# QK and exp cut into score chunks, set between AV and the MLP's matmuls

## The chip, the cores and the metric

The kernel runs on one core of a Trainium2 chip. A core has engines that run side by side, each with its own queue of instructions: TensorE (PE in the profile; its weight loads are the row PEld), VectorE (DVE), ScalarE (ACT), GpSimd (POOL), and SyncE (SP), which here only starts DMA transfers. They wait for one another through semaphores. Matmul results go to PSUM, everything else lies in SBUF.

The metric is the device time of one execution in microseconds (us). The time before is 412.74 us, the median of 6 runs (411.07 to 414.85).

## The reference

Grouped-query attention, then a gated MLP with a spatial mix. Cut to what is computed:

```python
# q: (8, 16, 384, 64)   k, v: (8, 4, 384, 64)    B, heads, S, D
k = np.repeat(k, 4, axis=1); v = np.repeat(v, 4, axis=1)
scores = (1 / np.sqrt(64)) * np.matmul(q, k.transpose(0, 1, 3, 2))
scores = scores - np.max(scores, axis=-1, keepdims=True)
attn = np.exp(scores)
attn = attn / (np.sum(attn, axis=-1, keepdims=True) + 1e-09)
x = np.matmul(attn, v).transpose(0, 2, 1, 3).reshape(8, 384, 1024)

h = np.maximum(x @ w_in, 0.0)                 # w_in: 1024 x 1024
u, v = h[..., :512], h[..., 512:]
v_n = (v - mean(v)) / np.sqrt(var(v) + 1e-06)
v_s = np.einsum('ts,bsd->btd', w_spatial, v_n) + b_spatial[None, :, None]
out = (u * v_s) @ w_out                       # w_out: 512 x 1024
```

## The kernel before

All 8 batches run on the one core, in a software pipeline of three stages: pass `it` does the attention of batch b0 = it, the normalization of the attention result and the first half of the MLP of batch b1 = it - 1, and the second half of the MLP of batch b2 = it - 2. A list `sched` gives the order of the pieces; a framework adds the semaphores. The order in the list is the order of preference: the framework may let a later instruction pass an earlier one on the same engine.

Heads are taken in pairs; a "unit" u is the heads 2u and 2u + 1, which share one k and v with the next or the previous unit. The scores stand transposed, 384 keys by 384 queries, as three chunks c of 128 keys. The pieces that matter:

```python
def psum_t(name):                      # every PSUM tile is one of 8 buffers
    return pp.tile([P, DH], FP32, name=name, tag="u", bufs=8)

def a_tr(b, u):                        # load and transpose q (and k, every second unit)
    ...
        nc.tensor.transpose(pkt[:, c * P:(c + 1) * P], k_sb[:, c], ident)      # x3
    nc.vector.tensor_copy(out=kT2, in_=pkt[:, 0:S])
    nc.gpsimd.dma_start(out=v_ext[:, :, 0:D], in_=v[b, hkv]...)                # 2 buffers
    ...
        nc.tensor.transpose(pqt[:, c * P:(c + 1) * P], q_sb[:, c], ident)      # x3
    nc.vector.tensor_copy(out=qT2, in_=pqt[:, 0:S])

def a_qk(b, u):                        # all scores of both heads, then all exps
    for c in range(NSC):               # NSC = 3
        for jj in range(2):            # D = 64 rows each, the two heads side by side
            lo = jj * D
            ps = psum_t(f"psc{jj}")
            pscs[jj][c] = ps
            nc.tensor.matmul(ps[:, 0:S], kT2[lo:lo + D, c * P:(c + 1) * P],
                             qT2[lo:lo + D, :], start=True, stop=True)
    for jj in range(2):
        p_sb = sb.tile([P, NSC, S], A, name="p_sb", tag="p_sb", bufs=8)
        for c in range(NSC):
            nc.scalar.activation(out=p_sb[:, c, :], in_=pscs[jj][c][:, 0:S],
                                 func=EXP, scale=scale)

def a_av(b, u):                        # v times exp, with a row of ones for the sum
    for jj in range(2):
        pav = psum_t("pav")
        for c in range(NSC):
            nc.tensor.matmul(pav[0:D + 1, 0:S], v_ext[:, c], p_sb[:, c],
                             start=(c == 0), stop=(c == NSC - 1))
        nc.vector.tensor_copy(out=st[b]["av"][0:D + 1, h, :], in_=pav[0:D + 1, 0:S])

def a_tail(b):                         # the sums of all heads, to 16 rows and back
    nc.sync.dma_start(out=dcol, in_=av_all[D:D + 1, :, :])
    nc.vector.reciprocal(out=rcol, in_=dcol)
    nc.sync.dma_start(out=rrow, in_=rcol)

def a_evac(b, hh):                     # four heads: broadcast 1/sum, multiply
    for h in range(hh, hh + 4):
        nc.gpsimd.partition_broadcast(R, rrow[:, h * S:(h + 1) * S], channels=D)
        nc.vector.tensor_tensor(out=st[b]["xT"][h // 2][lo:lo + D, :], ..., op=MULT)
```

`g_u` (x @ w_in, left half, 2 of 4 column blocks), `g_v` (right half, one of 3 row blocks), `g_n` (normalization), `g_s` (spatial mix, 2 of 4 blocks: matmuls `pvs`, then `gT` = `pvs` times u on VectorE) and `g_o` (@ w_out, one of 3 row blocks) are the MLP. The order of one pass:

```python
sched = [
    (a_tr, b0, 0), (a_tail, b1, None),
    (a_tr, b0, 1), (a_qk, b0, 0),
    (a_tr, b0, 2), (a_qk, b0, 1),
    (a_tr, b0, 3), (a_av, b0, 0), (a_qk, b0, 2), (a_evac, b1, 0),
    (a_tr, b0, 4), (a_av, b0, 1), (a_qk, b0, 3), (a_evac, b1, 4),
    (g_s, b2, 0),
    (a_tr, b0, 5), (a_av, b0, 2), (a_qk, b0, 4), (a_evac, b1, 8),
    (g_s, b2, 2),
    (a_tr, b0, 6), (a_av, b0, 3), (a_qk, b0, 5), (a_evac, b1, 12),
    (g_o, b2, 0),
    (a_tr, b0, 7), (a_av, b0, 4), (a_qk, b0, 6),
    (g_u, b1, 0), (g_o, b2, 1),
    (a_av, b0, 5), (a_qk, b0, 7),
    (g_u, b1, 2), (g_o, b2, 2),
    (a_av, b0, 6), (g_v, b1, 0), (g_v, b1, 1),
    (a_av, b0, 7), (g_v, b1, 2), (g_n, b1, None),
]
if it == 0:      # the first pass also loads the weights, and transposes w_spatial (9 blocks)
    sched = sched[0:1] + [(load_weights, 1, None)] + sched[1:9] + \
        [(load_wsp, 1, None)] + sched[9:]
```

The lines of the list are called steps 0 to 10 below (`g_s` and `g_o` belong to the step ahead of them): step s begins with the transposes of unit s.

Of the kernel before, what the change touches and what calls it, by code (L numbers as in the profile page):

```python
# [12 lines left out]
EXP = mybir.ActivationFunctionType.Exp  # L13
# [7 lines left out]
def kernel(  # L21
# [11 lines left out]
    nc = tc.nc  # L33
    P = 128
    B, HQ, S, D = q.shape
# [5 lines left out]
    NSC = S // P  # L41
    NDM = DM // P
    NDD = DH // P
    scale = float(D) ** -0.5
    A = FP16
# [3 lines left out]
    sb = ctx.enter_context(tc.tile_pool(name="sb", bufs=2))  # L49
    pp = ctx.enter_context(tc.tile_pool(name="pp", bufs=1, space=bass.MemoryType.PSUM))  # L50

    def psum_t(name):
        return pp.tile([P, DH], FP32, name=name, tag="u", bufs=8)
# [30 lines left out]
    st = {}  # L84

    def new_batch(b):
        st[b] = {
            "xT": [sb.tile([P, S], A, name=f"xT_{b}_{j}", tag="xT", bufs=2 * NDM)
                   for j in range(NDM)],
            "av": sb.tile([P, HQ, S], A, name="av_all", tag="av_all", bufs=2),  # L90
            "kv": {}, "qT": {}, "p": {}, "uT": [], "vn": [], "gT": [],
            "vsb": [], "acc": [],
        }
# [31 lines left out]
        nc.vector.tensor_copy(out=qT2, in_=pqt[:, 0:S])  # L125
        st[b]["qT"][u] = qT2

    def a_qk(b, u):
        kT2 = st[b]["kv"][u // 2][0]
        qT2 = st[b]["qT"].pop(u)  # L130
        pscs = [[None] * NSC, [None] * NSC]
        for c in range(NSC):
            for jj in range(2):
                lo = jj * D
                ps = psum_t(f"psc{jj}")
                pscs[jj][c] = ps
                nc.tensor.matmul(
                    ps[:, 0:S], kT2[lo:lo + D, c * P:(c + 1) * P], qT2[lo:lo + D, :],
                    start=True, stop=True,
                )  # L140
        for jj in range(2):
            p_sb = sb.tile([P, NSC, S], A, name="p_sb", tag="p_sb", bufs=8)
            st[b]["p"][2 * u + jj] = p_sb
            for c in range(NSC):
                nc.scalar.activation(out=p_sb[:, c, :], in_=pscs[jj][c][:, 0:S],  # L145
                                     func=EXP, scale=scale)

    def a_av(b, u):
        v_ext = st[b]["kv"][u // 2][1]
        for jj in range(2):  # L150
            h = 2 * u + jj
            p_sb = st[b]["p"].pop(h)
            pav = psum_t("pav")
            for c in range(NSC):
                nc.tensor.matmul(  # L155
                    pav[0:D + 1, 0:S], v_ext[:, c], p_sb[:, c],
                    start=(c == 0), stop=(c == NSC - 1),
                )
            nc.vector.tensor_copy(out=st[b]["av"][0:D + 1, h, :],  # L159
                                  in_=pav[0:D + 1, 0:S])  # L160

    def a_tail(b):
        av_all = st[b]["av"]
# [109 lines left out]
    for it in range(B + 2):  # L273
        b0 = it if it < B else None
        b1 = it - 1 if 1 <= it <= B else None
        b2 = it - 2 if it >= 2 else None
        if b0 is not None:
            new_batch(b0)
        sched = [
            (a_tr, b0, 0), (a_tail, b1, None),  # L280
            (a_tr, b0, 1), (a_qk, b0, 0),
            (a_tr, b0, 2), (a_qk, b0, 1),
            (a_tr, b0, 3), (a_av, b0, 0), (a_qk, b0, 2), (a_evac, b1, 0),
            (a_tr, b0, 4), (a_av, b0, 1), (a_qk, b0, 3), (a_evac, b1, 4),
            (g_s, b2, 0),
            (a_tr, b0, 5), (a_av, b0, 2), (a_qk, b0, 4), (a_evac, b1, 8),
            (g_s, b2, 2),
            (a_tr, b0, 6), (a_av, b0, 3), (a_qk, b0, 5), (a_evac, b1, 12),
            (g_o, b2, 0),
            (a_tr, b0, 7), (a_av, b0, 4), (a_qk, b0, 6),  # L290
            (g_u, b1, 0), (g_o, b2, 1),
            (a_av, b0, 5), (a_qk, b0, 7),
            (g_u, b1, 2), (g_o, b2, 2),
            (a_av, b0, 6), (g_v, b1, 0), (g_v, b1, 1),
            (a_av, b0, 7), (g_v, b1, 2), (g_n, b1, None),
        ]
        if it == 0:
            sched = sched[0:1] + [(load_weights, 1, None)] + sched[1:9] + \
                [(load_wsp, 1, None)] + sched[9:]
        for f, b, arg in sched:  # L300
            if b is None:
                continue
            if arg is None:
                f(b)
            else:
                f(b, arg)
# [30 lines left out]
```

The softmax here doesn't subtract the row's maximum and nothing guards it: scores larger than these inputs give would overflow.

## Time and profile before

| | before |
|---|---|
| median of 6 runs | 412.74 us |
| span of the profiled execution | 410.7 us |
| TensorE busy | 337.0 us |
| VectorE busy | 233.2 us |
| ScalarE busy | 213.3 us |
| GpSimd busy | 86.8 us |
| mean granted TensorE clock | 0.908 |

A page of the profile gives the busy time of each engine, then a chain of waits (the work that ended last, followed back), then groups of instructions. A group's line is: source line, engine, operation, output<-inputs, count, busy us and mean ns of one, idle us just before them and what ended it. Tiles are named as in the code: `psc` are scores, `p_sb` the exps, `pav` and `av_all` the AV result in PSUM and in SBUF, `pqt`/`qT` and `pkt`/`kT` the transposed q and k, `Rb` the broadcast reciprocals, `pw` the transposed blocks of w_spatial. The end of a matmul in the profile is modelled and matmuls overlap, so the distance between two starts tells more than a length. The granted clock is a share of full speed. "issue" is time in which an engine waited for nothing that the profile shows.

### The profile page before, as it was taken

The page shows a single profiled execution, that of the slowest core. Times are in us where ns is not written, and L with a number is a line of the kernel's source. Part 1 is how long each engine was busy: PE and PEld are TensorE (multiplying, and loading weights), DVE is VectorE, ACT ScalarE, POOL GpSimd, SP SyncE. Part 2 cuts the span into 40 slices and gives each one's busy share as a digit, 9 for nine tenths or more (in the row PEclk, how much of TensorE's full clock was granted, in tenths as well). Part 3 has the DMA queues.
Part 4 walks back from the last instruction along what each step waited for, and adds up shares of the span by engine and source line. Part 5 has one row for each costly group of instructions (what it writes and reads, how often), then busy time and mean ns, then how long its engine had stood idle before and what let it go on. Part 6 is the DMA issues. An engine that isn't in the chain of part 4 may idle for free.

```text
span 410.7 us, 5629 instructions
## 1 busy us (share of the span) xinstructions
PE 337.0 (82%) x1833; PEld 173.0 (42%) x1833; DVE 233.2 (57%) x593; ACT 213.3 (52%) x500; POOL 86.8 (21%) x179
## 2 busy tenths in 40 slices
PE   0444989898899789978998879978998889849875
PEld 0223545354455444543554445543554445413322
DVE  0211676759933994289617783289717973466240
ACT  1420978439563747557473737557473757303303
POOL 2510202601600070005200150005200340015000
PEclk9855999899999989999899689989899989968968
DMA  4995556116432634344423433354424402101204
GB/s 115 174 202 117 102 100 141 18 19 143 69 124 57 126 61 113 107 96 91 105 78 93 103 56 88 108 103 82 105 78 94 95 6 102 52 4 74 79 0 153
DMA packets 100108, 37.33 MB, mean 91 GB/s; under 512 B 90992, under 2 KB 92400, under 8 KB 100080
## 3 DMA queue, kind: packets, MB, share of 16 engines
q1 hardware_dynamic: 85520, 32.26, 29.9%
q0 software_dynamic: 14560, 4.72, 10.3%
q8 instruction: 14, 0.23, 0.2%
q14 instruction: 14, 0.11, 0.1%
HBM read 28.90 MB, written 12.58 MB: 101 GB/s over the span
## 4 chain that ended last, share of the span: by engine, by line
PE 59%; DVE 19%; ACT 7%; issue 5%; DMA 4%; SPq 3%; POOL 3%; POOLq 0%; ACTq 0%; DVEq 0%
PE pav L155 12%; PE pv L199 10%; PE pu L188 10%; PE po L261 9%; ACT p_sb L145 6%; DVE rcol L168 4%; PE pvs L247 4%; PE pkt L105 3%; PE pqt L123 3%; SPq L117 2%; PE pvs L251 2%; DVE gT L253 2%; DMA wsp_nat<-in_moe_w_spatial_dram 2%; DVE acc L207 1%; POOL Rb L177 1%
## 5 line engine op out<-in xcount | busy, mean ns | idle before, releaser
L159 DVE CAST av_all<-pav 65x384 f16<-65x384 f32 x128 | 67.0, 548 | 57.6 <-PE pav L155 53.7
L155 PE MATMUL pav<-p_sb,v_ext 128*65 128x384 f16 x384 | 81.3, 349 | 0.9 <-DVE av_all L159 0.7
L109 POOL DMA_DIRECT2D v_ext<-in_v_dram x32 | 25.1, 784 | 226.8 <-DVE av_all L159 56.2
L177 POOL PARTITION_BROADCAST Rb<-rrow x128 | 54.1, 543 | 50.9 <-DMA rrow<-rcol 28.2
L155 PEld LDWEIGHTS <-v_ext 128*65 128x65 f16 x384 | 46.2, 121 | 23.2 <-issue 2.6
L267 ACT COPY osb<-po 128x512 f32<-128x512 f32 x48 | 28.2, 593 | 38.2 <-PE po L261 37.6
L123 PE MATMUL pqt<-ident,q_sb 128*128 128x128 f32 x192 | 35.7, 306 | 7.6 <-DMA q_sb<-in_q_dram 7.6
L206 ACT ACTIVATE vsb<-pv 128x512 f16<-128x512 f32 x24 | 14.3, 597 | 40.6 <-PE pv L199 40.6
L123 PEld LDWEIGHTS pqt<-ident,q_sb 128*128 128x128 f32 x192 | 25.3, 158 | 14.4 <-issue 7.8
L207 DVE BATCH_NORM_STATS2 acc<-vsb 128x6 f32<-128x512 f16 x24 | 16.5, 687 | 22.9 <-ACT vsb L206 22.9
L261 PEld LDWEIGHTS <-gT 128*128 128x128 f16 x192 | 19.3, 102 | 23.3 <-issue 5.7
L105 PE MATMUL pkt<-ident,k_sb 128*128 128x128 f32 x96 | 20.2, 327 | 9.5 <-POOL ident masks.py:199 9.4
L193 ACT ACTIVATE uT<-pu 128x384 f32<-128x384 f32 x32 | 16.2, 514 | 11.2 <-PE pu L188 11.2
L113 DVE MEMSET v_ext<- 128x3 f16 x32 | 2.0, 61 | 34.4 <-DMA v_ext<-in_v_dram 34.4
L253 DVE TENSOR_TENSOR gT<-pvs,uT 128x384 f16<-128x384 f32 x32 | 16.7, 553 | 8.1 <-PE pvs L251 7.7
L247 PE MATMUL pvs<-w_spT_88,v_n 128*128 128x384 f16 x32 | 11.9, 372 | 11.2 <-DVE v_n L237 10.6
L105 PEld LDWEIGHTS pkt<-ident,k_sb 128*128 128x128 f32 x96 | 12.2, 160 | 20.1 <-POOL ident masks.py:199 9.4
L168 DVE RECIPROCAL rcol<-dcol 16x384 f16<-16x384 f16 x8 | 20.1, 2516 | 0.0
L261 PE MATMUL po<-w_out_sb_84,gT 128*128 128x512 f16 x48 | 19.4, 404 | 0.3
L261 PE MATMUL po<-w_out_sb_85,gT 128*128 128x512 f16 x48 | 19.2, 400 | 0.0
L261 PE MATMUL po<-w_out_sb_86,gT 128*128 128x512 f16 x48 | 19.0, 397 | 0.0
L261 PE MATMUL po<-w_out_sb_87,gT 128*128 128x512 f16 x48 | 18.9, 393 | 0.0
(1242 smaller groups left out, 740.1 us busy)
## 6 DMA issues: line engine op xcount, KB each, us to landing
q_sb<-in_q_dram SPq DMA_DIRECT2D x128, 96.0 KB, 2.5
out_dram<-osb SPq DMA_DIRECT2D x48, 256.0 KB, 2.0
k_sb<-in_k_dram SPq DMA_DIRECT2D x64, 96.0 KB, 2.5
v_ext<-in_v_dram POOLq DMA_DIRECT2D x32, 48.0 KB, 2.5
wsp_nat<-in_moe_w_spatial_dram SPq DMA_DIRECT2D x9, 64.0 KB, 2.0
w_in_sb_76<-in_moe_w_in_dram POOLq DMA_DIRECT2D x1, 256.0 KB, 4.6
w_in_sb_77<-in_moe_w_in_dram POOLq DMA_DIRECT2D x1, 256.0 KB, 6.3
w_in_sb_78<-in_moe_w_in_dram POOLq DMA_DIRECT2D x1, 256.0 KB, 7.5
```

Source lines behind the costliest of these rows:

```text
L105: nc.tensor.transpose(pkt[:, c * P:(c + 1) * P], k_sb[:, c], ident)
L109: nc.gpsimd.dma_start(out=v_ext[:, :, 0:D], in_=v[b, hkv].rearrange("(shi slo) d -> slo shi d", slo=P),)
L123: nc.tensor.transpose(pqt[:, c * P:(c + 1) * P], q_sb[:, c], ident)
L155: nc.tensor.matmul(pav[0:D + 1, 0:S], v_ext[:, c], p_sb[:, c], start=(c == 0), stop=(c == NSC - 1),)
L159: nc.vector.tensor_copy(out=st[b]["av"][0:D + 1, h, :], in_=pav[0:D + 1, 0:S])
L168: nc.vector.reciprocal(out=rcol, in_=dcol)
L177: nc.gpsimd.partition_broadcast(R, rrow[:, h * S:(h + 1) * S], channels=D)
L188: nc.tensor.matmul(pu[:, 0:S], w_in_sb[dmc][:, ddc * P:(ddc + 1) * P], st[b]["xT"][dmc], start=(dmc == 0), stop=(dmc == NDM - 1),)
L199: nc.tensor.matmul(pv, st[b]["xT"][dmc][:, sc * P:(sc + 1) * P], w_in_sb[dmc][:, DH:DFF], start=(dmc == 0), stop=(dmc == NDM - 1),)
L247: nc.tensor.matmul(pvs[:, 0:S], st[b]["vn"][sc][:, ddc * P:(ddc + 1) * P], w_spT[sc], start=(sc == 0), stop=False,)
L261: nc.tensor.matmul(po, st[b]["gT"][ddc][:, tcn * P:(tcn + 1) * P], w_out_sb[ddc][:, half * DH:(half + 1) * DH], start=(ddc == 0), stop=(dd ...
L267: nc.scalar.copy(out=osb, in_=po)
```

## The change

It cuts the QK block of a unit into its three score chunks. Each chunk computes the two heads' scores (two PSUM tiles and not six) and issues their two exps at once. A pass becomes eleven steps. In step s, chunk 0 of unit s - 1 comes after the transposes of unit s, then AV of unit s - 3, then chunk 1, then what the step has of the MLP and the normalization, then chunk 2. AV takes both heads in turn, chunk by chunk, into two PSUM tiles that are open together. The purpose is that scores, and with them the exps, come in a steadier flow, and that TensorE has AV and MLP work at hand while ScalarE works off the exps. In the first pass the weight loads stand ahead of the first transposes, and the transposes of w_spatial in step 2.

```diff
-    def a_qk(b, u):
+    def a_qk(b, uc):
+        u, c = uc
         kT2 = st[b]["kv"][u // 2][0]
-        qT2 = st[b]["qT"].pop(u)
-        pscs = [[None] * NSC, [None] * NSC]
+        if c == 0:
+            qT2 = st[b]["qT"].pop(u)
+            st[b]["p"][2 * u] = (sb.tile([P, NSC, S], A, name="p_sb", tag="p_sb",
+                                         bufs=8), qT2)
+            st[b]["p"][2 * u + 1] = (sb.tile([P, NSC, S], A, name="p_sb",
+                                             tag="p_sb", bufs=8), qT2)
+        qT2 = st[b]["p"][2 * u][1]
+        pscs = []
+        for jj in range(2):
+            lo = jj * D
+            ps = psum_t(f"psc{jj}")
+            pscs.append(ps)
+            nc.tensor.matmul(
+                ps[:, 0:S], kT2[lo:lo + D, c * P:(c + 1) * P], qT2[lo:lo + D, :],
+                start=True, stop=True,
+            )
+        for jj in range(2):
+            nc.scalar.activation(out=st[b]["p"][2 * u + jj][0][:, c, :],
+                                 in_=pscs[jj][:, 0:S], func=EXP, scale=scale)
+
+    def a_av(b, u):
+        v_ext = st[b]["kv"][u // 2][1]
+        pavs = [psum_t("pav"), psum_t("pav")]
         for c in range(NSC):
             for jj in range(2):
         ... (the old loop bodies of a_qk and a_av go)
+                    pavs[jj][0:D + 1, 0:S], v_ext[:, c], st[b]["p"][2 * u + jj][0][:, c, :],
+                    start=(c == 0), stop=(c == NSC - 1),
+                )
         for jj in range(2):
             h = 2 * u + jj
+            del st[b]["p"][h]
             nc.vector.tensor_copy(out=st[b]["av"][0:D + 1, h, :],
-                                  in_=pav[0:D + 1, 0:S])
+                                  in_=pavs[jj][0:D + 1, 0:S])
@@ the order (the old list goes)
+        def step(s, extra):
+            r = [(a_tr, b0, s) if s < 8 else None,
+                 (a_qk, b0, (s - 1, 0)) if 1 <= s <= 8 else None,
+                 (a_av, b0, s - 3) if 3 <= s - 3 + 3 <= 10 else None,
+                 (a_qk, b0, (s - 1, 1)) if 1 <= s <= 8 else None]
+            r += extra
+            r += [(a_qk, b0, (s - 1, 2)) if 1 <= s <= 8 else None]
+            return [x for x in r if x is not None]
+
+        sched = [(load_weights, 1, None)] if it == 0 else []
+        sched += step(0, [(a_tail, b1, None)])
+        sched += step(1, [])
+        sched += step(2, [(load_wsp, 1, None)] if it == 0 else [])
+        sched += step(3, [(a_evac, b1, 0)])
+        sched += step(4, [(a_evac, b1, 4), (g_s, b2, 0)])
+        sched += step(5, [(a_evac, b1, 8), (g_s, b2, 2)])
+        sched += step(6, [(a_evac, b1, 12), (g_o, b2, 0)])
+        sched += step(7, [(g_u, b1, 0), (g_o, b2, 1)])
+        sched += step(8, [(g_u, b1, 2), (g_o, b2, 2)])
+        sched += step(9, [(g_v, b1, 0), (g_v, b1, 1)])
+        sched += step(10, [(g_v, b1, 2), (g_n, b1, None)])
```

## The prediction, made before the changed kernel was run

> **What bounds the kernel now.** I read first the page (busy time, chain), then the waits of one steady batch, then busy time by stage, then the order of time around three places. Engine rows of the page:
>
> ```profile
> PE 337.0 (82%) x1833; PEld 173.0 (42%) x1833; DVE 233.2 (57%) x593; ACT 213.3 (52%) x500; POOL 86.8 (21%) x179
> ...
> PE 59%; DVE 19%; ACT 7%; issue 5%; DMA 4%; SPq 3%; POOL 3%; POOLq 0%; ACTq 0%; DVEq 0%
> ```
>
> The first line is busy time, the second the chain that ended last, by engine. TensorE is the nearest thing to a bound, but a fifth of the chain is VectorE, and exp on ScalarE is small in it (ACT 7%). The batches repeat every 44 us or so: the reciprocal starts at 92.5, 135.6, 179.6, 223.8, 271.3, 316.3 in the chain, 43.0 to 47.4 apart. So I cut one batch (133 to 177.2 us) into three stages and asked for busy time in each. Columns: stretch, its length, then busy us (and instructions) of PE, PEld, DVE, ACT, POOL, the granted clock, DMA share, GB/s.
>
> ```profile
> 133.00:138.50 5.50, 2.94 (x24) 1.88 (x21) 4.81 (x11) 3.00 (x7) 0.00 (x0) 1.00 0.66 128
> 138.50:157.70 19.20, 17.30 (x96) 8.56 (x97) 16.36 (x48) 12.27 (x32) 8.27 (x18) 0.91 0.44 86
> 157.70:177.20 19.50, 19.50 (x113) 10.39 (x112) 7.49 (x19) 11.09 (x24) 1.55 (x2) 1.00 0.31 94
> ```
>
> Third stage (steps 7 to 10, with the MLP's matmuls): TensorE has no gap, and ScalarE is 57% busy. Nothing but less TensorE work shortens it. First stage (steps 0 to 2): TensorE is half idle and VectorE 87% busy. Middle stage (steps 3 to 6): both lean on each other. The waits of TensorE in this batch (total, times, longest):
>
> ```profile
> PE psc_1731 L137 <- DVE qT_1688 L125: 1.5, 1, 1.5
> PE psc_1904 L137 <- DVE gT L253: 1.1, 1, 1.1
> PE psc_1690 L137 <- DVE qT_1673 L125: 1.1, 1, 1.1
> PE psc_1983 L137 <- ACT p_sb L145: 0.5, 1, 0.5
> ```
>
> The point: of 4.2 us, VectorE ends 3.7 and exp only 0.5. The change is aimed at the exp.
>
> [...] The QK matmuls use 64 rows, two heads side by side; everything around them uses 128. [...] Around one QK block:
>
> ```profile
> 208.47 1.14 PE L155 MATMUL pav<-p_sb,v_ext 128*65 128x384 f16 x6
> 209.54 0.33 PE L137 MATMUL psc_2718<-qT_2638,kT_2559 64*128 64x384 f16 x1
> ...
> 209.88 0.32 PE L137 MATMUL psc_2726<-qT_2638,kT_2559 64*128 64x384 f16 x1
> ...
> 210.14 0.34 PE L188 MATMUL pu<-xT_0_1645,w_in_sb_76 128*128 128x384 f16 x1
> ```
>
> Columns: start, length, engine, line, what. Matmuls of one mode start 0.16 us apart. The six AV matmuls span 1.14, so the last starts at 208.47 + 1.14 - 0.33 = 209.28; the first QK pair follows 0.26 later, 0.10 more than usual. The last pair starts at 209.88 and the next matmul at 210.14: again 0.26, 0.10 more. So a QK block costs about 0.2 us beside its own three pairs of 0.16.
>
> [...] In the trace the exps last 0.48 to 0.62 and start 0.37 apart, and there is one table load in the kernel. The change keeps 48 exps of the same shape per batch, so 48 x 0.37 = 17.8 us before and after: reordering them is free.
>
> [...]
>
> [...]
>
> **The change part by part.**
> (1) *Instructions.* Matmuls, exps and copies keep number and shape. Only order and buffers change.
>
> (2) *Mode switches.* Before, 8 QK blocks a batch. After, chunk 0 comes before AV, chunk 1 after it, chunk 2 after the extras. Steps 1 and 2 have neither AV nor extras on TensorE: one block each. Step 3 has AV only: two blocks. Steps 4 to 8 have three each, and chunk 2 of step 7 meets chunk 0 of step 8, as there is no transpose in between: 14. In all 18, so 10 more a batch. 10 x 0.2 = 2.0 us of TensorE a batch, 16 us over 8 batches if none is hidden. In the dense third stage: two blocks become five, 3 x 0.2 = +0.6 us, on the path. In the middle stage: seven more, +1.4 us, partly inside its waits.
>
> (3) *PSUM.* A block of six scores no longer asks for six of eight buffers at once, so waits like the 0.5 on p_sb should go. Against it, AV now opens both accumulators at its first two matmuls. In step 5 the tiles after the first pvs are pvs, two psc, pqt, two psc, pav, pav: the second pav is the eighth after, and must wait for gT, where before it was the fourth psc. That gT stands behind the VectorE work that follows AV of step 4:
>
> ```profile
> 143.75 0.77 POOL L109 DMA_DIRECT2D v_ext<-in_v_dram  x1 [10.91 <-PE psc_1835 L137]
> 144.56 4.89 POOL L177 PARTITION_BROADCAST Rb<-rrow  x12
> ...
> 148.43 1.02 DVE L253 TENSOR_TENSOR gT<-pvs,uT 128x384 f16<-128x384 f32 x2
> ...
> 149.04 0.32 PE L137 MATMUL psc_1904<-qT_1821,kT_1809 64*128 64x384 f16 x1 [1.10 <-DVE gT L253]
> ```
>
> GpSimd waits with the v_ext load until AV of step 4 has let go of the old v_ext, only then broadcasts, and VectorE multiplies eight heads (145.07 to 148.40, 3.3 us) before gT. The change does not touch this chain, and puts AV of step 4 behind one QK chunk, some 0.4 us later. So the stall stays, now with five or six AV matmuls (1.0 us) still to be done behind it. Middle stage by hand: +1.4 for the switches, about +1.0 for the stall, against about -2.4 for the PSUM waits named and the small ones that the chain shows (QK matmuls at 140.97, 141.35, 143.90 and 155.80 start 0.2 to 0.6 late, and pkt at 141.60 by 0.5). I call it 0, give or take 2 us a batch.
>
> (4) *Waits on qT in the first stage, 2.6 us.* Steps 0 to 2 have the same order as before (transposes, reciprocal, QK whole). The reciprocal of 2.5 us still stands ahead of the qT copy. No gain.
>
> (5) *Start.* The weight loads now come before the first v load, and the nine transposes of w_spatial come in step 2 and not after step 3. The trace before shows where the start waits:
>
> ```profile
> 23.15 2.13 PE L155 MATMUL pav<-p_sb,v_ext 128*65 128x384 f16 x6
> ...
> 37.19 0.45 PE L81 MATMUL pw<-ident,wsp_nat 128*128 128x128 f32 x1 [1.44 <-DMA wsp_nat<-in_moe_w_spatial_dram]
> ```
>
> The loads are the limit up to 37 us (the transpose before this one had waited 7.7 for another such tile). Six w_spatial tiles were issued from 29.8; after the change they may go some 6 us sooner. But the first v_ext goes behind the weights, as the second does now (issued at 22.0, its memset at 33.0), so the first AV moves from 23 to about 33 and leaves some 2 us of work behind the wait. I put the sum at -2, give or take 4.
>
> (6) *End.* The last two passes have no attention, and their order is unchanged: nothing.
>
> Sum: 412.7 + 8 x 0.6 (dense stage) + 0 (middle) + 0 (first) - 2 (start) = 415.5 us.
>
> **The rivals.**
> *A: the interleaving fills the gaps.* If all stalls of the middle stage went, with the clock dip after them, its 19.2 us would shrink by the 1.6 us of waits and 0.9 x 2 = 1.8 of clock (an estimate from the clock of 0.91), less 1.4 for switches: -2.0, plus 0.6 in the dense stage, -1.4 a batch. Over seven batches -10, with the start -12: 400 us. For it: ScalarE idles up to 4.6 us at a time (155.26). Against it: VectorE ends the largest waits, and it is 85% busy there.
> *B: the switches cost full price.* All 80 at 0.2: +16. A single pair may cost more: the pair at 155.80 is followed by its next matmul 0.38 later (156.18), 0.22 more than usual and not 0.10, so a block of one pair could cost 0.32, and 80 of them +26. Part hides in the middle stage: 425 to 430. For it: stage three has no gap. Against: half of the new blocks lie where TensorE waits anyway.
> *C: the start gets worse.* AV's wait for v_ext in front of all else: +4 to +6 alone.
>
> **Range and chances.** The middle stage at 2 us either way is worth up to 14 over seven batches, and the start 4; a mix of A and B gives 402 to 428 us, with 415.5 in the middle. Faster by over 2% (under 404.5) needs nearly all of A: 0.2. Slower by over 2% (over 421) needs B near its full price, or a longer stall on gT: 0.3. Within 2%: 0.5.
>
> **What would show it.** Stage three (steps 7 to 10) should grow from 19.5 to about 20.1 us, with each QK pair 0.26 or more from its neighbours; if it doesn't grow, the switch is cheaper than I think. In step 5, AV's second head should wait on gT in place of the fourth score; if no wait on gT is there, the order on VectorE or GpSimd has changed and A is right. The qT waits should stay at 2.6 us a batch, and ScalarE's busy time within a few us of 213. The first AV should move from 23 to over 30 us. I am wrong if the distance between two reciprocals falls under 42 us or rises over 46.

## The result: 0.8% faster, by clock and not by work

| | before | after |
|---|---|---|
| median | 413.45 us (20 runs) | 410.13 us (10 runs) |
| ratio to before, 95% interval | 1 | 0.9925 [0.989, 0.9961] |
| span of the profiled execution | 410.7 us | 407.4 us |
| mean granted TensorE clock | 0.908 | 0.924 |

Medians are of all executions; ratios and averages of lost clock leave out those more than 1.5% above the fastest of their kernel.

The prediction of 415.5 us was on the wrong side of no change, but within its range: the kernel is a little faster, within 2%. The page of the changed kernel, engine rows and chain by engine:

```profile
PE 338.0 (83%) x1833; PEld 163.8 (40%) x1833; DVE 232.5 (57%) x593; ACT 217.9 (53%) x500; POOL 86.0 (21%) x179
...
PE 59%; DVE 20%; issue 6%; POOL 4%; ACT 4%; DMA 3%; SPq 3%; POOLq 0%; ACTq 0%; DVEq 0%
```

Exp has shrunk in the chain (ACT 7% to 4%), VectorE has not. TensorE's busy time is what it was (337.0 and 338.0 us). So I cut the span at the first transposes of each pass (the first `pkt` behind the last `pv`), which needs no judgement about where a stage ends:

| stretch | before | after | difference |
|---|---|---|---|
| up to the third pass (first with all three stages) | 90.31 | 92.36 | +2.05 |
| five passes | 223.77 | 217.63 | -6.14 |
| last attention pass and the two behind it | 96.62 | 97.41 | +0.79 |
| sum | 410.7 | 407.4 | -3.3 |

The five passes lasted 43.02, 44.07, 44.21, 47.41 and 45.06 us before and 44.14, 42.98, 43.90, 43.63 and 42.98 after. The shortest of each are alike: 43.02 and 42.98. Both ran at a granted clock of 1.00 throughout. Busy time by stage in these two passes, first before and then after; columns as in the prediction:

```profile
89.98:95.48 5.50, 2.93 (x24) 1.88 (x21) 4.81 (x11) 3.00 (x7) 0.00 (x0) 1.00 0.68 132
95.48:113.08 17.60, 15.71 (x96) 7.72 (x97) 16.17 (x47) 12.26 (x32) 8.26 (x18) 1.00 0.47 92
113.08:133.12 20.04, 19.83 (x113) 10.41 (x112) 7.54 (x20) 11.11 (x24) 1.54 (x2) 1.00 0.30 92
```

```profile
136.17:141.67 5.50, 2.95 (x24) 1.89 (x21) 4.84 (x11) 3.00 (x7) 0.00 (x0) 1.00 0.62 115
141.67:159.08 17.41, 16.56 (x96) 7.52 (x96) 16.04 (x46) 12.41 (x30) 8.14 (x18) 1.00 0.50 99
159.08:179.27 20.19, 20.19 (x114) 10.15 (x114) 7.76 (x22) 11.59 (x25) 1.55 (x2) 1.00 0.29 91
```

Read the second line of each. In the middle stage TensorE idles 17.60 - 15.71 = 1.89 us before and 17.41 - 16.56 = 0.85 after: the interleaving does fill gaps, by 1.04 us. But the same 96 matmuls are busy 0.85 us longer, with seven more QK blocks and their changes from 128 rows to 64 and back (run 3 has the same 16.56, so AV's alternation is not the reason); 0.19 us is left. Cut at the first `pu` of a pass, the dense rest lasts 17.45 before and 18.08 after in every pass, +0.63, and the front of the two undisturbed passes 25.57 and 24.90, -0.67. In these two passes the change is neutral. Even that flatters it: 0.59 of the 0.67 us are a wait of this one pass before that goes away without any chunks (run 7).

The 6.14 us come from passes that were *not* undisturbed. One before and the same place after, in windows of 3.4 us:

```profile
147.00:150.40 3.40, 2.17 (x14) 0.58 (x11) 3.28 (x10) 2.22 (x6) 2.45 (x7) 1.00 0.25 58
150.40:153.80 3.40, 3.40 (x14) 2.02 (x14) 3.28 (x9) 0.29 (x1) 1.83 (x4) 0.57 0.00 0
153.80:157.20 3.40, 2.89 (x16) 1.31 (x15) 1.81 (x5) 1.94 (x6) 0.78 (x1) 0.93 0.74 130
```

```profile
146.00:149.40 3.40, 3.33 (x20) 1.38 (x18) 2.57 (x6) 2.40 (x6) 1.66 (x4) 1.00 0.82 178
149.40:152.80 3.40, 3.22 (x19) 1.50 (x20) 3.15 (x10) 2.55 (x6) 3.40 (x9) 1.00 0.44 70
152.80:156.20 3.40, 3.19 (x20) 1.70 (x19) 3.31 (x9) 1.72 (x4) 1.66 (x5) 1.00 0.11 26
```

Before, TensorE is busy 2.17 of 3.40 us (0.64) around its wait for `gT`, and in the window after it the granted clock is 0.57: half speed for nearly all of it, 14 matmuls in 3.40 us of busy time. After, no window of this stretch falls below 3.19 of 3.40 and the clock stays at 1.00. A half-speed stretch is 3.4 us long here, at a granted clock of 0.50, and loses 1.71 us of clock (the one behind this wait lasts from 150.85 to 154.27). Counted in the middle stages of the six passes from the third on: five of six have one before, none after. A second place, 2 to 5 us after the reciprocal starts, where TensorE waits for `qT`, has two before and three after, one of them twice as long in each.

The account of the five passes: excess over the undisturbed one before 223.77 - 5 x 43.02 = 8.67 us, from half-speed stretches of 11.96 us of lost clock (part of which hides in waits); after, 217.63 - 5 x 42.98 = 2.73, from two stretches (1.16 and 0.92) and one pass where a wait for `gT` is 1.0 and not 0.4 us (0.65). So -6.6 for the clock, +0.65 for that wait and -0.2 for all the rest. Of the 11.96 us lost before, 6.84 (four stretches) lie behind the waits of the middle stages, 5.12 behind those of the first stage; after, 0 and 3.41. The first stage has the same order in both kernels, so its share of the gain may be chance; the middle stage's is not, as every kernel with chunked scores and VectorE's order kept (eight profiles of six passes) has none there. The clock that is recorded for every execution says the same. Lost clock, which is the span times the share of the clock that was not granted, averages 34.8 us before (56 executions beside runs 1 to 4) and 31.5 after (10), 3.3 less; the spans differ by 2.6.

### The profile page after: what moved, and what is told of

The parts are those of the page before. It is cut to its first block, busy times and chain, and to the rows that moved or that the text cites. A ratio compares the mean times of both kernels' runs of the same rounds, so it can differ in the third digit from the quotient of the medians.

```text
span 407.4 us, 5663 instructions
## 1 busy us (share of the span) xinstructions
PE 338.0 (83%) x1833; PEld 163.8 (40%) x1833; DVE 232.5 (57%) x593; ACT 217.9 (53%) x500; POOL 86.0 (21%) x179
## 4 chain that ended last, share of the span: by engine, by line
PE 59%; DVE 20%; issue 6%; POOL 4%; ACT 4%; DMA 3%; SPq 3%; POOLq 0%; ACTq 0%; DVEq 0%
PE pav L156 12%; PE po L265 11%; PE pu L192 10%; PE pv L203 10%; DVE rcol L172 4%; ACT p_sb L148 3%; POOL Rb L181 3%; PE pqt L123 3%; DVE gT L257 2%; PE pvs L251 2%; DMA wsp_nat<-in_moe_w_spatial_dram 2%; SPq L117 2%; PE pkt L105 2%; DVE av_all L163 2%; POOL v_ext L109 1%
## 5 line engine op out<-in xcount | busy, mean ns | idle before, releaser
L163 DVE CAST av_all<-pav 65x384 f16<-65x384 f32 x128 | 65.9, 545 | 65.6 <-PE pav L156 62.3
L156 PE MATMUL pav<-p_sb,v_ext 128*65 128x384 f16 x384 | 78.6, 339 | 0.8 <-DVE av_all L163 0.6
L156 PEld LDWEIGHTS <-v_ext 128*65 128x65 f16 x384 | 39.5, 114 | 29.8 <-issue 13.9
L123 PE MATMUL pqt<-ident,q_sb 128*128 128x128 f32 x192 | 34.0, 295 | 0.1
L265 PEld LDWEIGHTS <-gT 128*128 128x128 f16 x192 | 18.9, 102 | 26.9 <-issue 9.3
L105 PE MATMUL pkt<-ident,k_sb 128*128 128x128 f32 x96 | 18.5, 306 | 9.9 <-POOL ident masks.py:199 9.7
L123 PEld LDWEIGHTS pqt<-ident,q_sb 128*128 128x128 f32 x192 | 23.4, 151 | 6.9 <-issue 3.7
L105 PEld LDWEIGHTS pkt<-ident,k_sb 128*128 128x128 f32 x96 | 11.3, 149 | 19.2 <-POOL ident masks.py:199 9.7
L81 PE MATMUL pw<-ident,wsp_nat 128*128 128x128 f32 x9 | 2.8, 391 | 19.4 <-DMA wsp_nat<-in_moe_w_spatial_dram 19.3
```

The costliest lines, as they stand in the source:

```text
L156: nc.tensor.matmul(pavs[jj][0:D + 1, 0:S], v_ext[:, c], st[b]["p"][2 * u + jj][0][:, c, :], start=(c == 0), stop=(c == NSC - 1),)
L265: nc.tensor.matmul(po, st[b]["gT"][ddc][:, tcn * P:(tcn + 1) * P], w_out_sb[ddc][:, half * DH:(half + 1) * DH], start=(ddc == 0), stop=(dd ...
```

## The experiments

Twelve kernels, each timed in several rounds beside the kernel before. Ratios are to that kernel, with 95% intervals. "Front" is from the first transposes of a pass to its first `pu`, in a pass at full clock. The changed kernel has 0.9925 and a front of 24.90.

### 1. The order of loads at the start

```diff
-        sched = [(load_weights, 1, None)] if it == 0 else []
-        sched += step(0, [(a_tail, b1, None)])
+        sched = step(0, [(a_tail, b1, None)])      # weights after the first transposes,
+        if it == 0: ...                            # w_spatial after step 3
```

> The changed kernel with the start of the kernel before: weight loads after the first transposes, w_spatial after step 3. Theory: the new start costs 2.1 us (first reciprocal at 94.6 and not 92.5), and the passes don't depend on it. So the first reciprocal goes back to 92.5 (give or take 0.5), the passes stay at 43.0 to 45, and the time falls by about 2 us, to a ratio of about 0.987 to the kernel before. Rival: the later start comes from the chunked steps 1 to 3 themselves; then the first reciprocal stays at 94 to 95 and the time does not move.

Measured: 410.3 us, 0.9906 [0.9868, 0.9944]; the reciprocal of the third pass, which the expectation calls the first, starts at 96.0 us. The start doesn't come back, so the load order alone doesn't cost the 2 us. The transposes of w_spatial wait for their loads in both kernels: the last ends at 39.7 us before and at 38.6 after.

### 2. Whole QK blocks in steps 7 and 8

```diff
+            if s in (7, 8):
+                r = [(a_tr, b0, s) if s < 8 else None, (a_av, b0, s - 3)]
+                r += [(a_qk, b0, (s - 1, c)) for c in range(3)] + extra
```

> The changed kernel with steps 7 and 8 as before: AV, then the whole QK block, then the MLP. Theory (each QK block costs 0.2 us of mode switches, and steps 7 to 10 have no gap): from the transposes of step 7 to the first transposes of the next pass 19.5 us and not 20.2, which is 0.7 less in each of 8 passes, 5 us in all, ratio about 0.98. Rival: the chunks pay for themselves there by feeding ScalarE steadily; then the exps pile up, TensorE waits, and the stretch stays at 20 us or more.

Measured: 409.34 us, 0.992 [0.9893, 0.9947]. From the first `pu` to the next pass it takes 17.45 us again, 0.63 less: the price of the switches is confirmed. But from the last transposes to the first `pu` it takes 2.5 us in place of 2.1: the six scores in one block span 0.90 us, and the last of them comes late. I take that for the wait for six PSUM tiles at once. Of 0.63 us, 0 to 0.3 a pass is left, and nothing in the median.

### 3. AV one head after the other

```diff
-        pavs = [psum_t("pav"), psum_t("pav")]
-        for c in range(NSC):
-            for jj in range(2):
+        for jj in range(2):
+            pav = psum_t("pav")
+            for c in range(NSC):
```

> The changed kernel with AV head by head, one accumulator after the other, as in the kernel before. Theory: the alternation of heads does nothing but lengthen six AV matmuls from 1.14 to 1.17 us; the ratio stays at 0.992 (0.987 to 0.997) and the undisturbed stretch from the first transposes to the first pu stays at 24.9 us. Rival: the alternation is what removed the PSUM waits of the middle stage; then that stretch goes back to 25.6 us.

Measured: 408.77 us, 0.9901 [0.9868, 0.9933]; front 24.61, no half-speed stretch in any middle stage, three of five passes at 42.70. So taking the heads in turn buys nothing and costs 0.29 us a pass; the gain lies in the spread scores. (In the medians the difference from the changed kernel is inside both intervals.)

### 4. Only the order of the exps

In the kernel before: scores in one block, but the six exps in order of chunks.

```diff
-        for jj in range(2):
-            for c in range(NSC):
+        for c in range(NSC):
+            for jj in range(2):
                 nc.scalar.activation(out=p_sb[...], in_=pscs[jj][c][:, 0:S], ...)
```

> The kernel before with one change: the exps of a QK block go chunk by chunk, in the order in which the scores are made, and not head by head. Theory: the middle stage gained because score tiles come free in the order in which they are taken, not because QK is spread out. Then the waits of the QK matmuls on p_sb (0.5 a pass) and on gT go here too, the undisturbed stretch from the first transposes to the first pu falls from 25.6 to about 24.9 us, steps 7 to 10 stay at 19.5, and the ratio is about 0.98. Rival: what helped is that only two scores at a time ask for buffers; then this order changes nothing, ratio 1.00.

Measured: 413.42 us, 1.0013 [0.9984, 1.0043]. The least busy 3.4 us of the middle stage (here from 9 us after the first transposes) are still 0.54 to 0.64 busy (before: 0.39 to 0.64), and half-speed stretches stand in two of six passes. The order of exps is worth nothing; it takes the scores in small portions between other matmuls. Whether what counts there is that fewer PSUM tiles are asked for at once, or that `g_s` comes ahead of the last chunk, no run separates.

### 5. A shorter reciprocal

After, with the sums on 128 partitions, so that the reciprocal takes 0.45 us and not 2.5.

```diff
-        dcol = sb.tile([HQ, S], A, ...)
+        dcol = sb.tile([P, HQ * S // P], A, ...)     # rcol likewise
```

> The changed kernel with the 16 x 384 sums laid over 128 partitions (48 each), so that the reciprocal of 2.5 us shrinks to about 0.4; the same numbers are computed. Theory: the wait of the QK matmuls on the second qT (1.5 us a pass) is the queue behind that reciprocal, and this idle stretch is where the clock still dips in the changed kernel. Then the wait of 1.5 goes, an undisturbed pass falls from 43.0 to about 41.4 us, the dips 2 to 5 us behind the reciprocal go, and the ratio to the kernel before is about 0.96. Rival: VectorE is full there anyway and the qT copy waits for something else next; the pass stays above 42.5, ratio 0.985.

Measured: 436.77 us, 1.0601 [1.0541, 1.0662]: far slower, which neither theory had. VectorE's order of time in the middle stage of one pass, and TensorE's waits in 49 us that hold this pass (total, times, longest):

```profile
249.71 0.55 DVE L107 CAST kT<-pkt 128x384 f16<-128x384 f32 x1
250.17 3.25 DVE L183 TENSOR_TENSOR xT<-av_all,Rb 64x384 f16<-64x384 f16 x8
253.45 0.56 DVE L125 CAST qT<-pqt 128x384 f16<-128x384 f32 x1
253.92 2.78 DVE L183 TENSOR_TENSOR xT<-av_all,Rb 64x384 f16<-64x384 f16 x7
256.63 1.01 DVE L163 CAST av_all<-pav 65x384 f16<-65x384 f32 x2
```

```profile
PE psc L143 <- DVE av_all L163: 2.4, 1, 2.4
PE psc L143 <- DVE qT L125: 2.2, 2, 1.1
```

In the changed kernel the sixteen multiplications come as eight, four and four, with copies between. Here 1/sum is ready sooner, and the framework sets the multiplications in one go ahead of the copies out of PSUM that TensorE needs (3.25 + 2.78 us, with one `qT` between). The wait of 1.5 us on the second `qT` is gone. But a wait of 1.1 on the `qT` between the multiplications is new (2.2 with the first of the pass), one on `av_all` is 2.4, and half-speed stretches follow: passes of 47 to 49 us. Lost clock averages 51.8 us where the changed kernel has 31.5, which is 20 of the 27 us between them. An instruction off the path was made faster, and it changed the order on the engine.

### 6 and 7. A third v_ext buffer, after and before

```diff
-        name="v_ext", tag="v_ext", bufs=2
+        name="v_ext", tag="v_ext", bufs=3
```

> The changed kernel with three v_ext buffers and not two, so that GpSimd no longer waits for AV of step 4 before the broadcasts. Theory: the waits on gT (0.7 us a pass) go, the undisturbed stretch from the first to the step-7 transposes falls from 22.8 to about 22.1 us, ratio about 0.98. Rival: VectorE is busy with qT, AV copies and normalization in that time, so the multiplications only push those back; the stretch stays at 22.8, ratio 0.99.

> The kernel before, unchanged but for three v_ext buffers. Theory: the stall on gT (1.1 us a pass) is what lets the clock dip about 15 us behind the reciprocal, in five of the six steady passes before and in none after. Then here the stall goes and these dips with it, and the kernel before comes to a ratio of about 0.985 without any chunks. Rival: the dips come from the scattered small waits of whole QK blocks; then they stay in at least four of six passes, and only the 1.1 us of the stall are won, or less.

Measured: 409.43 us, 0.993 [0.99, 0.996] after, and 411.56 us, 0.9957 [0.9934, 0.998] before. GpSimd's order of time in the changed kernel with the third buffer:

```profile
236.17 0.77 POOL L109 DMA_DIRECT2D v_ext<-in_v_dram  x1 [11.75 <-PE psc L143]
236.97 4.88 POOL L181 PARTITION_BROADCAST Rb<-rrow  x12
```

The load still waits 11.75 us for a score matmul, and the broadcasts stand behind it as in the prediction's lines. So it isn't the `v_ext` buffer that holds it, as I had read it; what does stays open. The wait for `gT` stays in both kernels (0.4 + 0.3 and 1.1 us), and in the changed one the stretch stays at 22.83 us in four of six passes, as the rival had it. Half-speed stretches remain in three of six middle stages of the kernel before.

The gain of 0.4% in run 7 is not clock: it loses 38.1 us of it on average (22 executions), the kernel before beside it 35.2 (29). So it lies in the work, and the trace shows one source. VectorE writes the ones into `v_ext` by a memset once v has landed. In the kernel before it sits idle ahead of this memset in step 6 for 1.1 to 2.1 us in each of the six steady passes; with the third buffer for at most 1.0, and in the changed kernel for at most 0.4. The `qT` copy of step 7 comes behind it. In the pass at full clock, before and in run 7:

```profile
113.56 0.06 DVE L113 MEMSET v_ext<- 128x3 f16 x1 [1.10 <-DMA v_ext<-in_v_dram]
...
114.80 0.56 DVE L125 CAST qT_1422<-pqt 128x384 f16<-128x384 f32 x1
```

```profile
115.25 0.06 DVE L113 MEMSET v_ext<- 128x3 f16 x1
...
115.38 0.56 DVE L125 CAST qT<-pqt 128x384 f16<-128x384 f32 x1
```

The passes begin at 90.31 and 91.85, so the copy comes after 24.49 and 23.53 us, the first `pu` after 25.57 and 24.98, and run 7's pass lasts 42.45 us. Held against that, the chunks cost 42.98 - 42.45 = 0.53 us a pass at full clock (0.25 with AV by head, 42.70), and the clock gives more than the 6.6 us above.

### 8. Three changes in one

AV by head (run 3), reciprocal on 128 partitions (5) and the third buffer (6) together.

> Chunks as in the changed kernel, AV head by head, the reciprocal over 128 partitions, three v_ext buffers. If the single terms add up (0.3 by head, 1.6 reciprocal, 0.7 v_ext, and no dips in the passes): an undisturbed pass of about 40.4 us, ratio 0.945. If VectorE is the limit of the first half of a pass, whatever is taken away: 41.5 us, ratio 0.965.

Measured: 421.98 us, 1.0234 [1.0189, 1.0279], passes of 45.4 to 46.8 us. The terms don't add; VectorE's order is again like that of run 5, with six and four multiplications ahead of a copy out of `pav`.

### 9. The reciprocal behind the second qT copy

Run 3, with the tail emitted after the second transposes.

```diff
-        sched += step(0, [(a_tail, b1, None)])
-        sched += step(1, [])
+        sched += step(0, [])
+        s1 = step(1, [])
+        sched += s1[:1] + [(a_tail, b1, None)] + s1[1:]     # if s1 is not empty
```

> Attention values one head after the other, and the normalization's start (reciprocal and what follows it) emitted after the second transpose of the pass instead of before it. Theory: the 2.5-us reciprocal is what keeps the second qT copy, and with it TensorE, waiting 1.5 us; with the reciprocal behind that copy the wait goes from 1.5 to below 0.5, the front of an undisturbed pass falls from 24.6 to about 23.6 us and the clock dips 2 to 5 us after the reciprocal become rarer; the median falls by 5 to 9 us from 408.8, to 400-404. Rival: the next kT and qT copies stand behind the same 2.5 us and TensorE waits for them instead; the front stays within 0.3 us of 24.6 and the median at 407-411.

Measured: 403.32 us, 0.9794 [0.9746, 0.9842]; front 23.83, three of five passes at 41.9. VectorE's order of time at the start of a pass, in the changed kernel and here:

```profile
224.98 0.54 DVE L125 CAST qT_2889<-pqt 128x384 f16<-128x384 f32 x1
...
225.53 2.51 DVE L172 RECIPROCAL rcol<-dcol 16x384 f16<-16x384 f16 x1
...
227.98 0.54 DVE L125 CAST qT_2904<-pqt 128x384 f16<-128x384 f32 x1
```

```profile
136.08 0.54 DVE L125 CAST qT<-pqt 128x384 f16<-128x384 f32 x1
...
136.62 0.52 DVE L125 CAST qT<-pqt 128x384 f16<-128x384 f32 x1
...
137.13 2.53 DVE L171 RECIPROCAL rcol<-dcol 16x384 f16<-16x384 f16 x1
```

The second copy no longer stands 3.0 us behind the first but 0.54. TensorE's waits in a whole pass, the changed kernel and then this one:

```profile
PE psc_1733 L143 <- DVE qT_1688 L125: 1.5, 1, 1.5
PE psc_1692 L143 <- DVE qT_1673 L125: 1.1, 1, 1.1
PE pvs L251 <- DVE gT L257: 0.4, 1, 0.4
PE psc_1985 L143 <- DVE gT L257: 0.3, 1, 0.3
```

```profile
PE psc L143 <- DVE qT L125: 1.6, 2, 1.1
PE po L264 <- DVE gT L256: 0.3, 1, 0.3
```

The 1.5 us have become 0.6 (1.64 less 1.05 in the order of time), and `gT` holds the middle stage for 0.3 and not 0.7. TensorE is busy 4.25 of the first 5.50 us where it was 2.95:

```profile
134.15:139.65 5.50, 4.25 (x30) 2.28 (x27) 4.81 (x11) 3.20 (x8) 0.00 (x0) 1.00 0.67 129
```

One half-speed stretch is left in six passes. The theory holds, with 0.78 us a pass in place of 1.0 and a wait of 0.6 in place of less than 0.5. Over all executions the span is 4.6 us shorter than run 3's (401.7 and 406.3 on average), of which 1.3 are lost clock; the rest is work. By ratio it is 1.1% against run 3, more than the 0.75% of the change itself, though the intervals overlap. It moves one call by a few lines.

### 10. The same, with the reciprocal on 32 partitions

The expectation says 64 partitions; the kernel went from 16 to 32, with 192 elements on each, as stated there.

```diff
-        dcol = sb.tile([HQ, S], A, ...)
+        dcol = sb.tile([2 * HQ, S // 2], A, ...)            # rcol likewise
```

> As the run before it, with the sums laid over 64 partitions, so that the reciprocal handles 192 elements a partition and takes some 1.25 us instead of 2.5. Theory: the wait behind it is halved too, front 0.5 to 1 us shorter than with the late reciprocal alone, median 398-403. Rival: the earlier reciprocal brings the multiplications ahead of the copies of attention values on VectorE, as with 128 partitions, and TensorE waits for those copies in the middle stage: passes above 44 us, median 412 or more.

Measured: 429.27 us, 1.0419 [1.0373, 1.0465], passes of 45.7 to 47.9 us. The rival was right. The reciprocal takes 1.33 us, and VectorE's order turns as in run 5:

```profile
158.20 2.88 DVE L182 TENSOR_TENSOR xT<-av_all,Rb 64x384 f16<-64x384 f16 x7
161.11 0.56 DVE L125 CAST qT<-pqt 128x384 f16<-128x384 f32 x1
161.58 1.56 DVE L182 TENSOR_TENSOR xT<-av_all,Rb 64x384 f16<-64x384 f16 x4
163.18 0.55 DVE L162 CAST av_all<-pav 65x384 f16<-65x384 f32 x1
```

TensorE waits 1.7 us for `av_all` in this pass. Only the reciprocal's shape differs from run 9, by 1.2 us of VectorE a pass, and the kernel is 26 us slower. Lost clock makes 17 of these (45.2 us on average, and 28.3 in run 9).

### 11 and 12. The first pass, whole, and with its old order of loads

Run 3 with whole score blocks in the first pass; then run 9 with these and, in that pass, the order of loads of the kernel before (run 1).

```diff
+            if it == 0:
+                r = [(a_tr, b0, s) if s < 8 else None, (a_av, b0, s - 3) if s >= 3 else None]
+                if 1 <= s <= 8:
+                    r += [(a_qk, b0, (s - 1, c)) for c in range(3)]
+                return [x for x in r + extra if x is not None]
```

> Attention values one head after the other, and in the first pass, where no MLP work stands between them, the score blocks whole as before the change. Theory: the 1.7 us that the changed kernel loses up to the first pass with MLP work come from the chunked order of the first pass; its end (first transposes of pass 1) moves from 55.5 back to about 54 us, median 407. Rival: it is the second pass, chunked and also without a full MLP, and the first stays at 55 or more; median 408-409.5.

> Everything that helped, in one kernel: attention values one head after the other, the normalization's start behind the second transpose, and the first pass in full as in the kernel before: score blocks whole and, other than in the run with the first pass's blocks whole alone, also its order of loads (weights after the first transposes, spatial weights after step 3). Theory: order of loads and chunks together make the 1.7 us of the start, which neither gave back alone; first transposes of pass 1 at 53.5-54.2 us instead of 55.5, undisturbed front 23.8 us as with the late normalization, median 399-403. Rival: the start stays at 55.4 whatever its order, so it is set by something else that varies with the build; then the median is that of the late normalization, 402-405.

Measured: 406.46 us, 0.9855 [0.9801, 0.9909], and 400.13 us, 0.97 [0.9661, 0.9739], 12.6 us less than the kernel before beside it (412.76) and the fastest here. Run 11's first pass ended no sooner; run 12's did, as its theory had it. Its chain by engine, to be held against VectorE's 20% and TensorE's 59% in the changed kernel:

```profile
PE 62%; DVE 14%; ACT 8%; POOL 6%; DMA 5%; issue 4%; SPq 1%; POOLq 0%; ACTq 0%
```

The first transposes of the second pass, in order of time; one line of the kernel before, of the changed one, of run 11 and of run 12:

```profile
53.81 0.49 PE L105 MATMUL pkt<-ident,k_sb 128*128 128x128 f32 x3
```

```profile
55.54 0.49 PE L105 MATMUL pkt<-ident,k_sb 128*128 128x128 f32 x3
```

```profile
55.48 0.49 PE L105 MATMUL pkt<-ident,k_sb 128*128 128x128 f32 x3
```

```profile
54.06 0.49 PE L105 MATMUL pkt<-ident,k_sb 128*128 128x128 f32 x3
```

The old order of loads alone gave 55.4 (run 1), whole blocks alone 55.48, both 54.06: either change of the start is enough to lose the 1.5 us, and only taking back both regains it. Of the 1.5 us, 0.7 are left by the third pass (91.87, and 92.56 in run 9), and the profiled spans differ by the same 0.7 (398.3 and 399.0). The medians differ by 3.2. Over the six executions of each, spans average 398.7 and 401.7 us and lost clock 25.4 and 28.3, so the difference goes with half speed; why run 12 has less of it stays open. Run 11's median lies 2.3 us below run 3's with no sooner start. Its lost clock is less, too (26.9 and 29.6 us on average), but the intervals overlap widely.

## Why the prediction was right and wrong

That 415.5 us came so near is partly luck: the middle stage came out 1.9 us a pass better than forecast, over five passes 9.3 us, and the start 4 us worse. By its own steps:

**(2) Mode switches (from 128 rows to 64 and back): right.** Predicted 0.2 us a QK block and +0.6 in the dense stage. Measured, around the lone pair of chunk 1 in step 8 (order of time, changed kernel):

```profile
166.26 1.17 PE L156 MATMUL pav<-p_sb,v_ext 128*65 128x384 f16 x6
167.36 0.33 PE L143 MATMUL psc_2118<-qT_2030,kT_1951 64*128 64x384 f16 x1
...
167.62 0.34 PE L192 MATMUL pu<-xT_0_1037,w_in_sb_76 128*128 128x384 f16 x1
```

The last AV matmul starts at 166.26 + 1.17 - 0.33 = 167.10, the pair 0.26 later, the next matmul 0.26 after that: 0.1 on either side, for a block of one pair as for one of three. The dense stage went from 19.49 (pass from 133.33) to 20.19 us: +0.70 for three blocks, 0.23 each. The 0.32 that rival B gave a lone pair falls, and run 2 took the dense stage's price back by itself (17.45 us from the first `pu` for 18.08).

**(3) PSUM and the middle stage: the term that failed.** I put it at 0 us a pass. Measured over the five passes, the time ahead of the first `pu` fell by 6.14/5 + 0.63 = 1.86 us a pass. It splits into 6.6/5 = 1.32 for the half speed that vanished, 0.67 for the undisturbed front (0.59 of it the wait ahead of the memset, run 7), and 0.65/5 = 0.13 given back in the pass with the longer wait. Three things were wrong in it. First, I had let the stall on `gT` stay as it was, and so the half clock behind it: I had seen both (1.10 us of waiting, then a granted clock of 0.80 from 151.9 to 157.7) and named the gain in rival A only. The stall did not stay: 1.1 us on one score before, 0.4 and 0.3 after. Second, I had the second `pav` of step 5 wait for `gT`, by counting eight PSUM tiles in strict turn, since `psc_1904`, the eighth tile after the first `pvs`, had waited 1.10 us for `gT` before. It did not; the wait sits further on, at the second `pvs`:

```profile
150.33 1.16 PE L156 MATMUL pav<-p_sb,v_ext 128*65 128x384 f16 x6
...
153.00 0.32 PE L251 MATMUL pvs<-w_spT_88,v_n 128*128 128x384 f16 x1 [0.38 <-DVE gT L257]
```

AV runs through without a gap 2.7 us before that `pvs` starts, while `gT` only starts at 152.40. So work lies in front of the wait, not behind it, and the buffers are not given out in strict turn. Third, the chain from the `v_ext` buffer over GpSimd to `gT`: runs 6 and 7 took the buffer away as a reason, and the load went on waiting. What the chain is in truth stays open.

Rival A had the steady passes nearly right: -1.4 a pass as stated, -1.23 measured (6.14/5), and it had the clock in it. But it let every wait of the middle stage go (1.6 us), and 0.7 us of `gT` stayed. At the start it failed like the forecast, with -2 for +2.05.

**(4) qT waits: right.** 2.6 us before and after, by the lines under run 9. What the prediction took as a given, run 9 showed to be the best place to work on.

**(5) Start: wrong in sign.** Predicted -2 give or take 4, measured +2.05. The first AV went from 23.15 to 38.91 us (predicted: over 30), but the last transpose of w_spatial ended only 1.1 us sooner, and the work put off behind it was not made up for. Runs 1, 11 and 12 show that the chunks alone or the order of loads alone are enough to cost 1.5 us of it.

**(6) End:** predicted nothing; +0.79 together with the last attention pass, which has a half-speed stretch of twice the usual length after (314.5 to 321.3) and a single one before (331.8 to 335.2). ScalarE's busy time, 217.9, is within a few us of 213, as stated.

What is shown and what isn't: that the gain is time at half clock which vanished is shown by the passes' account, and that it takes scores in portions and not the order of exps or of AV by runs 3 and 4. That TensorE's idle time brings on the half clock is a reading. In the three kernels with whole scores (before, runs 4 and 7) the least busy 3.4 us of the middle stage are 0.39 to 0.64 busy in all 18 passes, and ten have such a stretch; in the eight with chunks they are 0.65 to 0.92 busy in 48 passes, and none has. But no run varied the idle time alone.

## What to carry to other kernels

Before counting what an interleaving fills, cut the trace by passes and compare those at full clock: here they were alike or, held against run 7, half a microsecond worse, and the whole gain was in the clock of the others. Then look at what stands ahead of a small copy on the engine that ends the largest wait: moving one 2.5-us instruction behind that copy gave at least as much as the whole rewrite of the score blocks. And when such an instruction is shortened instead, read the order on its engine anew: it changed both times (runs 5 and 10), and 1.2 us less work a pass cost 26 us.

## What the hardware showed that I had not expected

Half speed behind a stretch in which TensorE had worked most of the time: in the windows shown under the result, TensorE was 0.64 busy in the 3.4 us ahead, never idle for more than the 1.1 us of its longest wait there, and then lost 1.71 us of clock in one 3.4-us stretch.

The changes of the clock keep to a grid. In both profiles, before and after, the time from one change of the granted clock to the next is always a whole number of steps of 3.413 us. Before, the half-speed stretches of the six passes start at 150.85, 195.22, 225.94, 243.01, 273.73, 287.38 and 331.76 us, which are 13, 9, 5, 9, 4 and 13 steps apart. In the first stage, which passes are hit goes with where these steps fall. Somewhere in it TensorE is only 0.43 busy over 3.4 us, in each of 54 passes (before, after, runs 1 to 4, 6, 7 and 11), but a step often does not fall just there. Two passes of the kernel before, each with the least busy step of its first stage and the step behind it:

```profile
178.16:181.57 3.41, 1.85 (x16) 0.98 (x14) 3.41 (x5) 1.64 (x6) 0.00 (x0) 1.00 0.58 132
181.57:184.98 3.41, 2.39 (x19) 1.36 (x20) 3.34 (x14) 3.03 (x10) 0.00 (x0) 1.00 0.66 150
```

```profile
270.32:273.73 3.41, 1.47 (x12) 0.84 (x12) 3.41 (x6) 2.14 (x6) 0.00 (x0) 1.00 0.71 162
273.73:277.14 3.41, 2.92 (x13) 1.65 (x14) 2.54 (x11) 2.86 (x8) 0.00 (x0) 0.50 0.57 130
```

Behind the step with 1.85 of 3.41 us (0.54) the clock stays at 1.00, behind the one with 1.47 (0.43) it is 0.50. In 14 of the 54 passes the least busy step has 0.43 to 0.49, and half speed follows every time; in the other 40 it has 0.50 to 0.61, and half speed follows twice. It is no full rule: in the middle stage before, steps of 0.64 or 0.70 were followed by half speed in five passes, and one of 0.64 in the pass from 90.31 was not; in runs 9 and 12 one step each of 0.75 to 0.76 was.
